# A transformer block with dilated local attention on one Trainium2 core: q and k columns in steps of four, V from a doubled scratch, halved reductions for late tiles, and a new order

## The chip, the cores and the metric

The kernel runs on one core of a Trainium2 chip. Its engines work on their own lists of instructions and meet at semaphores: TensorE (PE; its weight loads are listed apart as PEld), VectorE (DVE), ScalarE (ACT), GpSimd (POOL) and SyncE (SP), which here issues nearly all DMAs. The metric is device time of one execution in microseconds (us). Three runs of the kernel before gave 239.56, 240.42 and 240.76; their median, 240.42 us, is the time before.

## What is computed

One adaLN-conditioned block over S = 2048 tokens of D = 512: layer norm and modulation, attention with 32 heads of 16 dims in which each token sees itself and seven earlier tokens two apart, a gated residual, a second layer norm and modulation, a SwiGLU FFN of width 1792, a second gated residual.

```python
qkv = (h @ wqkv) ...                 # (B, H, S, 16) each
idx = pos[:, None] - arange(8) * 2   # window 8, dilation 2
logits = einsum('bhsd,bhswd->bhsw', q, kg) * scale   # masked where idx < 0
o = einsum('bhsw,bhswd->bhsd', softmax(logits), vg)
x = x + ga * (o @ wo)
h = layernorm(x) * (1 + cb) + sb
x = x + gb * ((silu(h @ w1) * (h @ w3)) @ w2)
```

All data is bf16; sums on TensorE are in float32.

## The kernel before

**How the work is staged.** The tokens are 16 tiles T of 128. A layer norm on DVE (statistics, L579) and ACT or DVE (normalization) is followed by a transpose and the modulation (`ln_T`; on PE for early groups, by DMA transpose and L648 on ACT for late ones). The normalized tokens lie as h with features on partitions. `proj_qk` computes q and k of up to four tiles as four chunks `ft` of 128 features on partitions by tokens (L722), with wqkv as the stationary operand; ACT copies them to the q buffer (L730) and to `kT` (L733, L734). `proj_v` computes V with tokens on partitions (L749), ACT copies it with dims ahead of heads (L759), and a DMA stores it in DRAM, in `v_scratch_dram`, one row of 512 per token.

**Attention of a tile** runs on DVE and PE:
- `logits`: one product of q with eight shifted views of kT (L780, 128x4096, the op called pq). PE sums the 16 features of a head with 0/1 matrices `E_sb[:, ft, :]`, one for each chunk, since chunk ft holds heads 8 ft to 8 ft + 7: four chunks by four column tiles of the array, 16 matmuls of 256 columns (L791, the op lg), out on partitions as (token block, head).
- `shift`, `exps`, `softmax`, for two tiles at a time: maximum (L803) and subtraction (L808) on DVE, exponential on ACT (L821), sum (L833), reciprocal (L835), normalization (L836) and a 32x32 block transpose (L840) on DVE, which puts (token, offset) on partitions.
- `values`: four DMAs of 256 KB per tile fetch V again, as 16 token pairs by 8 offsets on the partitions and two tokens in a row (128 packets of 2 KB each). DVE multiplies it by the weights in place (L862, 128x4096, the op av). PE sums the eight offsets with the 0/1 matrices `ind[:, r]` (8 matmuls of 512 columns in four column tiles, L871, the op ac), ACT copies (L877), a DMA transposes, PE applies wo (L895, the op wo), and DVE adds to x (L899, the op rs).

**The rest.** The second layer norm (`ln_sums`: L610, L614 and L625 on ACT, L620 and L621 on POOL, L622), then the FFN in groups of tiles [0, 1], [2, 3], [4..7], [8..11], [12..15]: `ffn_unit` is four matmuls for the gate and four for the up part (L911), silu on ACT (L917), the product on DVE (L922 or, in the last group, L925); `ffn_w2` the second matmul (L953, and L941 for the last two tiles), then L969 adds x and a DMA stores the result. DVE also scales wo and w2 by the gates (L987, L996). The gates come from two small matmul groups and a cast on DVE (`gate`, L555, L561).

**What sets the order.** `_build` makes 1151 operations, each with an engine, a planner's cost in ns (C_PQ, C_RED, `c_mm` and so on), what it reads and writes, and a key. `ORDER` (L1018) is a written-out permutation of them; each engine works its operations in that order, SP its DMAs too. `SLOTS` (L1064) says which buffer each value takes: the products and the fetched V share four buffers and two places in memory that is free by then (their names in the profile, sb_pq, sb_vsh, sb_vshq, sb_vshx, tell the buffer and not the use). `synchronize` puts in the waits that follow from both. Both lists were searched on the planner's costs outside the kernel. So an operation is found in the trace by its line and by its place in its engine's list.

Of the kernel before, what the change touches and what calls it, by code (L numbers as in the profile page):

```python
# [10 lines left out]
P = 128  # L11
# [10 lines left out]
PAD = 16  # L22
# [52 lines left out]
class Program:  # L75
# [41 lines left out]
    def dma(self, out, in_, key, packets, r=(), w=(), part=(), after=(), eng="sp", cost=450, group=None, transpose=False,  # L117
            store=False, again=False, pre=()):
        nc = self.nc

        def fn(e):
            a = out() if callable(out) else out
            b = in_() if callable(in_) else in_
            with nc.allow_non_contiguous_dma(reason="layout"):
                for pa, pb in pre:
                    e.dma_start(pa, pb).then_inc(o.inc[0], 16)
                return e.dma_start(a, b, transpose=True) if transpose else e.dma_start(a, b)
# [3 lines left out]
        ns = 600 if transpose else each * ((PACKET if pre == () and not SHIFTED else 84) if again else packet_ns(size)) + 170 * len(pre)  # L131
        o = self.op(eng, fn, cost, key, r=r, w=w, part=part, after=after, dma=(each, ns, *((900, 200) if store else (1300, 600))))
        o.count = 1 + len(pre)
# [119 lines left out]
C_PQ, C_RED, C_ACC, C_TINY = 2203, 440, 864, 90  # L253
# [18 lines left out]
SHIFTED = False  # L272
NWARM = 15
DMA_T = (4, 2)
AVCOL = frozenset(range(16))
# [5 lines left out]
def _build(p, A_x, A_wqkv, A_wo, B_w1, B_w3, B_w2, c, w_mod, out):  # L281
# [15 lines left out]
    kT = sb([P, KT, PAD + S], bf, "kT")  # L297
# [16 lines left out]
    E_sb = sb([P, KT, H], bf, "E")  # L314
    ones = sb([P, 512], bf, "ones")
    ind = sb([P, 2, 16, 2], bf, "ind")
# [27 lines left out]
    zrow = at([PAD, D], bf, "zrow", 25600)  # L344
# [7 lines left out]
    v_dram = nc.dram_tensor("v_scratch_dram", (PAD + S, D), bf)  # L352
    skew = nc.dram_tensor("skew_dram", (NT, 16, 4160), bf) if SHIFTED else None
# [20 lines left out]
    def held(pool, items):  # L374

        vals = []
        for i, item in enumerate(items):
# [9 lines left out]
    vc, vident, vcst, vE, vind, vbefore = (Val(n) for n in ("const", "ident", "cst", "E", "ind", "before"))  # L387
# [11 lines left out]
    p.op("pool", lambda e: e.memset(E_sb[:], 1.0), 150, k, w=[vE])  # L399
    p.op("pool", lambda e: e.affine_select(out=E_sb[:], in_=E_sb[:], compare_op=ALU.is_ge, fill=0.0, base=0,  # L400
                                           pattern=[[128, KT], [-16, H]], channel_multiplier=1), 320, k, w=[vE])
    p.op("pool", lambda e: e.affine_select(out=E_sb[:], in_=E_sb[:], compare_op=ALU.is_ge, fill=0.0, base=15,
                                           pattern=[[-128, KT], [16, H]], channel_multiplier=-1), 320, k, w=[vE])
    p.op("pool", lambda e: e.memset(ind[:], 0.0), 100, k, w=[vind])
    for r in range(2):
        p.op("pool", lambda e, r=r: e.memset(ind[:, r, :, r], 1.0), 100, k, w=[vind])
    for edge, mult in ((0, 1), (W - 1, -1)):
        p.op("pool", lambda e, edge=edge, mult=mult: e.affine_select(
            out=ind[:], in_=ind[:], compare_op=ALU.is_ge, fill=0.0, base=edge, pattern=[[0, 2], [-W * mult, 16], [0, 2]],
            channel_multiplier=mult), 250, k, w=[vind])  # L410
# [6 lines left out]
    p.op("dve", lambda e: e.memset(kT[:, :, 0:PAD], 0.0), 120, k, w=[vkpad])  # L417
# [35 lines left out]
    p.dma(v_dram[0:PAD, :], zrow[:], ("load", 11), (16, 1024), r=[vzrow] + wm_hold, w=[vvpad], store=True)  # L453
# [52 lines left out]
    def first_modulation(part):  # L506
# [16 lines left out]
        if not part:  # L523
# [3 lines left out]
            def kbias(e):  # L527
                for ft in range(KT):
                    for t in range(KT):
                        ins = e.matmul(bank(vb)[:, ft:ft + 1], wqkv[:, t, D + ft * P:D + (ft + 1) * P], sab[:, t:t + 1],  # L530
                                       start=(t == 0), stop=(t == KT - 1))
# [176 lines left out]
    def proj_qk(gi, Ts, kind, vh):  # L708
# [7 lines left out]
        for ft in range(KT):  # L716
# [3 lines left out]
            def mm(e, ts, ft=ft, vp=vp):  # L720
                for t in ts:
                    ins = e.matmul(bank(vp)[:, 0:n], wqkv[:, t, kind * D + ft * P:kind * D + (ft + 1) * P], vh.at[:, t, 0:n],  # L722
# [5 lines left out]
            def ev(e, ft=ft, vp=vp):  # L728
                if kind == 0:
                    return e.activation(dstv.at[:, ft, at0:at0 + n], bank(vp)[:, 0:n], ACT.Copy, scale=SCALE)  # L730
                to = kT[:, ft, PAD + 512 * cch + at0:PAD + 512 * cch + at0 + n]
# [11 lines left out]
    def proj_v(T, tt, vh):  # L743
# [19 lines left out]
        p.dma(v_dram[PAD + T * P:PAD + (T + 1) * P, :], lambda: vt.at[:], k, (128, 1024), r=[vt], w=[vd], cost=400, store=True)  # L763
# [5 lines left out]
    def logits(Ts):  # L769

        vl = Val("ps_l", psum)
        for i, T in enumerate(Ts):
# [4 lines left out]
            def prod(e, T=T, cch=cch, tt=tt, vp=vp):  # L777
                in0 = bass.AP(vq[cch].at, tt * P, [[KT * 512, P], [0, W], [512, KT], [1, P]])
                in1 = bass.AP(kT, PAD + T * P, [[KT * (PAD + S), P], [-DIL, W], [PAD + S, KT], [1, P]])
                return e.tensor_tensor(bass.AP(vp.at, 0, [[8 * D, P], [KT * P, W], [P, KT], [1, P]]), in0, in1, ALU.mult)  # L780

            prods[T] = p.op("dve", prod, C_PQ, ("pq", T), r=[vq[cch]] + ks + (q_hold if cch < 2 else []), w=[vp], lock=True)
            def red(e, i=i, T=T, vp=vp):
                c0 = vl.at * 512 + i * W * 32
                if T == 0:
# [3 lines left out]
                for ft in range(KT):  # L789
                    for q in range(4):  # L790
                        ins = e.matmul(PALL[32 * q:32 * q + 32, c0:c0 + W * 32], E_sb[:, ft, :], bass.AP(vp.at, ft * P + 8 * q, [[W * KT * P, P], [KT * P, W], [32, 4], [1, 8]]),  # L791
                                       start=(ft == 0 and (T > 0 or q > 1)), stop=(ft == KT - 1), tile_position=(0, 32 * q))
                return ins

            p.op("pe", red, C_RED + (110 if T == 0 else 0), ("lg", T), r=[vp, vE] + ([vbefore, vc] if T == 0 else []), part=[vl], tiled=True)
# [32 lines left out]
    def softmax(Ts, vl, ve, vx_):  # L828
# [7 lines left out]
        p.op("dve", lambda e: e.tensor_tensor(ve.at[0][:, 0:n], bass.AP(PALL, bank(vl).offset, [[8 * 512, P], [W * 32, n], [1, 32], [32, W]]),  # L836
                                              bass.AP(ve.at[2], 0, [[64, P], [32, n], [1, 32], [0, W]]), ALU.mult),
# [272 lines left out]
```

## Time and profile before

| | |
|---|---|
| runs | 239.56, 240.42, 240.76 us |
| median | 240.42 us |
| span of the profiled execution | 237.7 us (237.65 by its windows) |
| around the span, against the median | 2.77 us |
| matmuls (PE records) | 1665, busy 229.9 us |
| DVE | 284 instructions, busy 169.8 us |
| ACT | 311 instructions, busy 156.4 us |
| DMA | 38.31 MB, mean 161 GB/s |

The execution's own time is not listed apart from its span; what lies around the span is put at the difference to the median. The profile is one execution; a group of it lists line, engine, operation, output<-input, count, then busy us and mean ns of one, then the engine's idle time just before and what ended it. "Busy" of PE is modelled: a 512-column matmul is drawn 379 ns long although the next one starts some 216 ns later. In the windows view each engine has its busy time in that stretch. In the chain of waits each piece is what the next one waited for.

### The profile page before, as it was taken

What the parts mean: (1) busy time and instruction counts of PE and PEld (TensorE: products, weight loads), DVE (VectorE), ACT (ScalarE), POOL (GpSimd) and SP (SyncE); (2) the same over time, 40 slices, a digit from 0 to 9 for tenths busy, and PEclk for the clock granted to TensorE, in tenths of its full rate; (3) what the DMA queues carried; (4) which work ended last, traced back from release to release, by engine and by line L of the source; (5) the groups of instructions that cost most, each with busy time, mean ns of one, the idle gap of its engine ahead of it and who ended that gap; (6) DMA issues with size and microseconds to landing.
All of it is one profiled execution on the core that took longest, in us unless ns stands there. A gap on an engine that the chain in (4) does not pass through costs nothing.

```text
span 237.7 us, 4314 instructions
## 1 busy us (share of the span) xinstructions
PE 229.9 (97%) x1665; PEld 120.7 (51%) x1689; DVE 169.8 (71%) x284; ACT 156.4 (66%) x311; POOL 23.1 (10%) x55
## 2 busy tenths in 40 slices
PE   7899998999999999999999999999999999999996
PEld 2667543544568855754434444444344444444454
DVE  4789998999999999999999847379134424042722
ACT  2289798899989987683689799444757926133100
POOL 8323050001001000030000021000001100000000
PEclk9999999999999999999999999999999999999999
DMA  6999999989999977693897484330032142000002
GB/s 185 341 352 351 238 274 179 188 221 297 327 261 273 285 181 223 139 261 69 205 330 116 124 229 105 103 117 0 3 90 88 44 77 80 0 0 0 3 0 88
DMA packets 44731, 38.31 MB, mean 161 GB/s; under 512 B 19736, under 2 KB 36008, under 8 KB 44712
## 3 DMA queue, kind: packets, MB, share of 16 engines
q1 hardware_dynamic: 44656, 38.04, 63.3%
q8 instruction: 13, 0.21, 0.4%
q14 instruction: 6, 0.05, 0.1%
q10 hardware_dynamic: 56, 0.01, 0.0%
HBM read 29.63 MB, written 4.21 MB: 142 GB/s over the span
## 4 chain that ended last, share of the span: by engine, by line
PE 68%; DVE 12%; DMA 7%; ACT 7%; issue 3%; POOL 1%; SPq 1%; DVEq 0%
PE pall L911 38%; PE pall L953 13%; PE pall L722 5%; DMA sb_wo<-in_A_wo_dram 5%; PE pall L895 4%; DVE sb_vsh L862 3%; PE pall L941 3%; DMA sb_wm_s<-in_w_mod_dram 2%; PE pall L871 2%; PE pall L749 2%; ACT sb_h L648 1%; ACT sb_xn L614 1%; PE pall L791 1%; DVE sb_pq L780 1%; DVE sb_pq L862 1%
## 5 line engine op out<-in xcount | busy, mean ns | idle before, releaser
L911 PE MATMUL pall<-sb_h,sb_w 128*128 128x512 bf16 (+1 forms) x554 | 99.6, 336 | 0.5 <-issue 0.2
L911 PEld LDWEIGHTS pall<-sb_h,sb_w 128*128 128x128 bf16 x560 | 52.2, 98 | 47.1 <-ACT sb_sg L917 5.2
L917 ACT ACTIVATE sb_sg<-pall 128x512 bf16<-128x512 f32 (+1 forms) x70 | 33.9, 516 | 29.6 <-PE pall L911 28.6
L953 PE MATMUL pall<-sb_w,sb_hh 128*128 128x512 bf16 x190 | 43.4, 379 | 0.3
L722 PE MATMUL pall<-sb_h,sb_wqkv 128*128 128x512 bf16 (+1 forms) x157 | 30.4, 336 | 1.3 <-ACT sb_v L759 0.8
L953 PEld LDWEIGHTS pall<-sb_w,sb_hh 128*128 128x128 bf16 x196 | 18.9, 98 | 22.7 <-issue 0.4
L921 ACT ACTIVATE sb_hh<-pall 128x256 bf16<-128x256 f32 (+1 forms) x56 | 26.8, 497 | 3.4 <-PE pall L911 3.0
L922 DVE TENSOR_TENSOR sb_hh<-sb_sg,sb_hh 128x256 bf16<-128x256 bf16 (+1 forms) x56 | 17.7, 351 | 12.8 <-ACT sb_hh L921 12.8
L969 DVE TENSOR_TENSOR sb_o<-pall,sb_x 128x512 bf16<-128x512 f32 (+3 forms) x18 | 10.9, 627 | 18.5 <-PE pall L953 13.7
L722 PEld LDWEIGHTS pall<-sb_h,sb_wqkv 128*128 128x128 bf16 x160 | 14.6, 98 | 14.0 <-ACT sb_v L759 1.3
L925 DVE TENSOR_TENSOR sb_hh<-sb_sg,pall 128x512 bf16<-128x512 bf16 x14 | 9.1, 684 | 16.0 <-PE pall L911 15.9
L648 ACT ACTIVATE sb_h<-sb_h,sb_modc 128x512 bf16<-128x512 bf16 x16 | 11.7, 806 | 11.2 <-DMA sb_h<-sb_xn 11.2
L620 POOL TENSOR_SCALAR sb_rs<-sb_var 128x2 f32<-128x2 f32 x8 | 3.4, 427 | 144.4 <-ACT sb_xn L614 144.4
L862 DVE TENSOR_TENSOR sb_pq<-sb_pq,sb_al 128x4096 bf16<-128x4096 bf16 x7 | 15.8, 2285 | 1.0 <-DMA sb_pq<-v_scratch_dram 1.0
L862 DVE TENSOR_TENSOR sb_vsh<-sb_vsh,sb_al 128x4096 bf16<-128x4096 bf16 x7 | 15.9, 2281 | 0.0
L749 PE MATMUL pall<-sb_wqkv,sb_h 128*128 128x512 bf16 x59 | 15.2, 379 | 0.3 <-issue 0.2
L895 PE MATMUL pall<-sb_wo,sb_ot 128*128 128x512 bf16 x60 | 14.9, 379 | 0.6 <-issue 0.5
L673 ACT ACTIVATE sb_h<-pall,sb_modc 128x256 bf16<-128x256 bf16 (+1 forms) x20 | 12.2, 659 | 2.7 <-DVE sb_modc L522 1.8
L780 DVE TENSOR_TENSOR sb_vsh<-sb_q,sb_kT 128x4096 bf16<-128x4096 bf16 x6 | 13.6, 2286 | 0.4 <-ACT sb_q L730 0.4
L625 ACT ACTIVATE sb_xn<-sb_x,sb_nb,sb_rs 128x512 bf16<-128x512 bf16 x16 | 12.4, 818 | 1.9 <-DVE sb_nb L622 1.7
L614 ACT ACTIVATE sb_xn<-sb_x,sb_nm 128x512 bf16<-128x512 bf16 x16 | 11.4, 716 | 2.7 <-DVE sb_nm L610 2.7
L899 DVE SCALAR_TENSOR_TENSOR sb_x<-pall,sb_x 128x512 bf16<-128x512 f32 x16 | 10.7, 678 | 2.9 <-PE pall L895 2.7
(111 smaller groups left out, 254.5 us busy)
## 6 DMA issues: line engine op xcount, KB each, us to landing
sb_pq<-v_scratch_dram SPq DMA_DIRECT2D x28, 256.0 KB, 6.8
sb_vsh<-v_scratch_dram SPq DMA_DIRECT2D x28, 256.0 KB, 5.0
sb_w<-in_B_w_dram SPq DMA_DIRECT2D x6, 512.0 KB, 6.9
sb_w<-in_B_w_dram SPq DMA_DIRECT2D x6, 384.0 KB, 5.9
v_scratch_dram<-sb_v SPq DMA_DIRECT2D x16, 128.0 KB, 5.8
out_dram<-sb_o SPq DMA_DIRECT2D x14, 128.0 KB, 1.8
sb_wqkv<-in_A_wqkv_dram SPq DMA_DIRECT2D x6, 256.0 KB, 6.2
sb_x<-in_A_x_dram SPq DMA_DIRECT2D x3, 512.0 KB, 7.7
```

The costliest lines, as they stand in the source:

```text
L614: p.op("act", lambda e, vn=vn, T=T: e.activation(vn.at[:], x_sb[:, T, :], ACT.Square, bias=nm[:, T, :], scale=D ** -0.5, accum_out=var[:, ...
L648: return e.activation(vh.at[:, ft, 0:n * P], vh.at[:, ft, 0:n * P], ACT.Identity, bias=modc[:, 8 * which + ft:8 * which + ft + 1], scale=m ...
L722: ins = e.matmul(bank(vp)[:, 0:n], wqkv[:, t, kind * D + ft * P:kind * D + (ft + 1) * P], vh.at[:, t, 0:n], start=(t == ORDER[0]), stop=(t ...
L749: ins = e.matmul(bank(vp), vh.at[:, t, tt * P:(tt + 1) * P], wqkv[:, t, 2 * D:3 * D], start=(t == ORDER[0]), stop=(t == ORDER[-1]))
L780: return e.tensor_tensor(bass.AP(vp.at, 0, [[8 * D, P], [KT * P, W], [P, KT], [1, P]]), in0, in1, ALU.mult)
L862: return e.tensor_tensor(v_w, v_w, a_w, ALU.mult)
L895: ins = e.matmul(bank(vy), vt.at[:, ft, :], wo[:, ft, :], start=(ft == 0), stop=(ft == KT - 1))
L911: ins = e.matmul(bank(vp)[:, 0:n], wt[:, t, fi * P:(fi + 1) * P], vh.at[:, t, 0:n], start=(t == 0), stop=(t == KT - 1))
L917: p.op("act", lambda e: e.activation(vt.at[:, 0:n], bank(vgp)[:, 0:n], ACT.Silu), c_act(n), k, r=[vgp], w=[vt], table="silu")
L921: p.op("act", lambda e: e.activation(vh_.at[:, 0:n], bank(vup)[:, 0:n], ACT.Copy), c_act(n), k, r=[vup], w=[vh_])
L922: p.op("dve", lambda e: e.tensor_tensor(vh_.at[:, 0:n], vt.at[:, 0:n], vh_.at[:, 0:n], ALU.mult), 60 + n * 69 // 128, k, r=[vt], w=[vh_], ...
L953: ins = e.matmul(bank(vz), vhh[fi].at[:, tt * P:(tt + 1) * P], w2[:, fi, :], start=(fi == 0), stop=(fi == NF - 1))
```

## The change

1. **q and k columns in steps of four.** The stationary operand of chunk ft is now columns ft, ft + 4, ft + 8 and so on of wqkv in place of 128 neighbouring ones; the bias matmuls of the first group likewise (L530). Partition p of each chunk then holds head p // 4. One 128x32 matrix `ind` (1 where p // 4 is the head) takes the place of the four in `E_sb` and of the two in `ind[:, r]`; five of eight building operations on POOL go.
2. **V as 32 tokens by 4 offsets.** The scratch has two columns of 512 per row: row r holds V of token r and of token r + 32, so each store writes every row twice (256 packets of 1 KB in place of 128). Each of the four loads per tile is 32 tokens by 4 offsets on partitions with two token blocks in a row, still 128 packets of 2 KB. Slots 0 to 3 of the fetched V are offsets 0 to 3, slots 4 to 7 offsets 4 to 7.
3. **The normalization** (L836) is done per tile, two instructions of 256 elements a partition in place of one of 512, writing in the order that the transpose needs; the block transpose then reads and writes contiguous rows.
4. **Halves added on VectorE.** For tiles 12 to 15 (`PREL`) a DVE add folds chunks 2 and 3 of the products onto 0 and 1, and the reduction has 8 matmuls in place of 16. For tiles 10 to 15 (`PREA`) a DVE add folds offsets 4 to 7 of the weighted V onto 0 to 3, and the reduction has 4 matmuls in place of 8.
5. **A new searched order** and new buffer slots for the now 1164 operations. Read as lists: PE starts with 14 warm-up matmuls in a row, does all q and k of tiles 0 to 3 ahead of most of V; SP fetches the second gate's weights early; DVE has both gate casts ahead of the first product; the logits of tiles 14 and 15 come after the value reduction of tile 11, the folded products of tiles 13 to 15 ahead of it.

Branches that were never taken (`SHIFTED`, tiles outside `AVCOL`) are removed with it.

```diff
-                    ins = e.matmul(bank(vp)[:, 0:n], wqkv[:, t, kind * D + ft * P:kind * D + (ft + 1) * P], vh.at[:, t, 0:n],
+                    ins = e.matmul(bank(vp)[:, 0:n], wqkv[:, t, kind * D + ft:(kind + 1) * D:KT], vh.at[:, t, 0:n],
...
-        p.dma(v_dram[PAD + T * P:PAD + (T + 1) * P, :], lambda: vt.at[:], k, (128, 1024), r=[vt], w=[vd], cost=400, store=True)
+        p.dma(bass.AP(v_dram, (PAD + T * P) * 2 * D, [[2 * D, P], [D - 64 * D, 2], [1, D]]),
+              lambda: bass.AP(vt.at, 0, [[D, P], [0, 2], [1, D]]), k, (256, 1024), r=[vt], w=[vd], cost=400, store=True)
...
+            if T in PREL:
+                def fold(e, vp=vp):
+                    lo, hi = (bass.AP(vp.at, j * 2 * P, [[8 * D, P], [KT * P, W], [1, 2 * P]]) for j in range(2))
+                    return e.tensor_tensor(lo, lo, hi, ALU.add)
+
+                p.op("dve", fold, C_ADD, ("pq", T), w=[vp], lock=True)
...
+                last = (2 if T in PREL else KT) - 1
-                for ft in range(KT):
+                for ft in range(last + 1):
                     for q in range(4):
-                        ins = e.matmul(PALL[32 * q:32 * q + 32, c0:c0 + W * 32], E_sb[:, ft, :], bass.AP(vp.at, ft * P + 8 * q, [[W * KT * P, P], [KT * P, W], [32, 4], [1, 8]]),
+                        ins = e.matmul(PALL[32 * q:32 * q + 32, c0:c0 + W * 32], ind[:],
+                                       bass.AP(vp.at, ft * P + 8 * q, [[W * KT * P, P], [KT * P, W], [32, 4], [1, 8]]),
...
-        p.op("dve", lambda e: e.tensor_tensor(ve.at[0][:, 0:n], bass.AP(PALL, bank(vl).offset, [[8 * 512, P], [W * 32, n], [1, 32], [32, W]]),
-                                              bass.AP(ve.at[2], 0, [[64, P], [32, n], [1, 32], [0, W]]), ALU.mult),
+        for i in range(n):
+            def norm(e, i=i):
+                src = bass.AP(PALL, bank(vl).offset + i * W * 32, [[8 * 512, P], [128, 2], [1, 32], [32, 4]])
+                rec = bass.AP(ve.at[2], i * 32, [[64, P], [0, 2], [1, 32], [0, 4]])
+                dst = bass.AP(ve.at[0], i * W * 32, [[2 * W * 32, P], [128, 2], [4, 32], [1, 4]])
+                return e.tensor_tensor(dst, src, rec, ALU.mult)
...
-        for q in range(4):
-            p.dma(lambda q=q: vv.at[:, 2 * q:2 * q + 2, :],
-                  bass.AP(v_dram, (PAD + T * P + 32 * q) * D, [[2 * D, 16], [-DIL * D, W], [1, 2 * D]]), ("vl", T), (128, 2048),
+        for wh in range(2):
+            for c in range(2):
+                p.dma(lambda s=4 * wh + 2 * c: vv.at[:, s:s + 2, :],
+                      bass.AP(v_dram, (PAD + T * P + 64 * c - 4 * DIL * wh) * 2 * D, [[2 * D, 32], [-DIL * 2 * D, 4], [1, 2 * D]]),
...
+        if T in PREA:
+            p.op("dve", lambda e: e.tensor_tensor(vv.at[:, 0:4, :], vv.at[:, 0:4, :], vv.at[:, 4:8, :], ALU.add), C_ADD, ("av", T),
+                 w=[vv], lock=True)
...
+            parts = 1 if T in PREA else 2
+            for wh in range(parts):
+                for q in range(4):
+                    ins = e.matmul(b[32 * q:32 * q + 32, :], ind[:], vv.at[:, 4 * wh + q, :], start=(wh == 0), stop=(wh == parts - 1),
+                                   tile_position=(0, 32 * q))
```

More of the change, by code (lines that the diff above doesn't have):

```diff
@@ L21 @@
 NF = F // P
-PAD = 16
+PAD = 32
+KPAD = 16
 EPS = 1e-5
@@ L891, in values @@
+        p.op("act", lambda e: e.activation(va.at[:], bank(vo), ACT.Copy), c_act(512), ("ac", T), r=[vo], w=[va])
+        p.dma(lambda: vt.at[:], lambda: va.at[:], ("ac", T), (128, 1024), r=[va], w=[vt], cost=1250, transpose=True)
         vy = Val("ps_y", psum)
```

101 lines of the change are left out of this document (35 added, 66 removed), and 120 rows, old and new, of tables (ORDER, SLOTS).

## The prediction, made before the result

> **What bounds the kernel now.** I read the page first: its busy shares and the strip of 40 slices (5.94 us each).
>
> ```profile
> span 237.7 us, 4314 instructions
> ...
> PE 229.9 (97%) x1665; PEld 120.7 (51%) x1689; DVE 169.8 (71%) x284; ACT 156.4 (66%) x311; POOL 23.1 (10%) x55
> ```
> ```profile
> PE   7899998999999999999999999999999999999996
> ...
> DVE  4789998999999999999999847379134424042722
> ```
>
> TensorE (PE) is busy from end to end, so less matmul work can pay. But VectorE (DVE) stands at 8 or 9 from slice 2 to slice 22 (to 137 us) and only then falls off. Its 71% is a mean over a full half and an idle one. So I cut the span with the windows view: at the first q·k product (23.60), at the value reduction of tile 11 (132.90), and at the start of the FFN of tiles 8 to 11 (157.01). Columns: length, then busy time of PE, PEld, DVE, ACT, POOL.
>
> ```profile
> 0.00:23.60 23.60, 21.11 (x198) 13.14 (x201) 16.92 (x58) 13.67 (x32) 10.55 (x35) 1.00 0.96 308
> 23.60:132.90 109.30, 107.02 (x951) 61.30 (x961) 106.43 (x139) 89.99 (x185) 8.51 (x12) 1.00 0.94 223
> 132.90:157.01 24.11, 23.84 (x121) 10.38 (x117) 13.53 (x34) 19.28 (x34) 2.15 (x4) 1.00 0.59 157
> ```
>
> In the middle stretch PE is idle 2.28 us of 109.30 and DVE 2.87 us: two engines are full side by side. Behind it PE is full and DVE half idle. The clock is 1.00 throughout. The cut at 132.90 is where they meet, as the timeline shows:
>
> ```profile
> 130.56 2.29 DVE L862 TENSOR_TENSOR sb_pq<-sb_pq,sb_al 128x4096 bf16<-128x4096 bf16 x1
> ```
> ```profile
> 132.90 0.61 PE L871 MATMUL pall<-sb_pq,sb_ind 128*32 128x512 bf16 x8
> ```
>
> DVE ends tile 11's weighting at 132.85; PE starts on it at 132.90. There is no slack there. The chain of waits says the same 18 us earlier (start, length, what):
>
> ```profile
> 112.24 2.21 DVE sb_vshx L780
> ...
> 114.50 0.62 PE pall L791 x16
> ...
> 132.19 0.87 PE pall L791 x32
> 133.06 0.46 PE pall L871 x8
> ...
> 134.49 5.18 PE pall L911 x24
> ...
> 170.13 1.84 PE pall L871 x32
> ```
>
> Up to here the chain is on DVE, from here nearly all on PE. So a change that takes work from PE and gives it to DVE has to be booked on both sides of 132.9.
>
> **The change, part by part.**
>
> *Halved reductions (PE).* Tiles 12 to 15 get 8 in place of 16 matmuls for the logits, tiles 10 to 15 get 4 in place of 8 for the values. In the chain 32 logit matmuls (two tiles) take 0.87, so 0.435 a tile; 32 value matmuls (four tiles) take 1.84, so 0.46 a tile. Saved: 4 x 0.22 + 6 x 0.23 = 2.26 us.
>
> *Folds and split (DVE).* Ten adds of 128 x 2048 bf16 are new, and each of the eight normalizations becomes two of 256 elements. Rows of the groups:
>
> ```profile
> L996 DVE TENSOR_TENSOR sb_w<-sb_w,sb_gb_bc 128x2048 bf16<-128x2048 bf16 x2 | 2.4, 1191 | 0.0
> L836 DVE TENSOR_TENSOR sb_attn<-pall,sb_ssum 128x512 bf16<-128x512 f32 x8 | 5.5, 687 | 0.1
> L969 DVE TENSOR_TENSOR sb_o<-pall,sb_x 128x256 bf16<-128x256 f32 x2 | 0.8, 420 | 1.1 <-PE pall L941 1.1
> L922 DVE TENSOR_TENSOR sb_hh<-sb_sg,sb_hh 128x512 bf16<-128x512 bf16 x28 | 10.6, 419 | 12.8 <-ACT sb_hh L921 12.8
> L803 DVE TENSOR_REDUCE sb_mx<-pall 128x64 f32<-128x512 f32 x8 | 5.4, 680 | 0.0
> L808 DVE TENSOR_TENSOR pall<-pall,sb_mx 128x512 f32<-128x512 f32 x8 | 5.6, 697 | 0.1
> L899 DVE SCALAR_TENSOR_TENSOR sb_x<-pall,sb_x 128x512 bf16<-128x512 f32 x16 | 10.7, 678 | 2.9 <-PE pall L895 2.7
> ```
>
> One operation overlaps the next by about 0.08 (a product lasts 2.29 but takes 2.21 in the chain), so a fold costs 1.19 - 0.08 = 1.11 and a split 2 x 0.34 - 0.61 = 0.07. In all DVE gains 10 x 1.11 + 8 x 0.07 = 11.7 us. A fold could take between half a product (1.10) and the two-tensor row (1.19); I take 1.11.
>
> *The new order*, read as two lists. I counted which operations stand on each side of tile 11's value reduction.
> DVE, from the first product to tile 11's weighting and its fold: six of the ten folds (6.7), six splits (0.4), two more FFN products (0.7), but one pair of maximum and subtraction fewer (1.2), one residual add fewer (0.6) and some tiny ones (0.2): 5.8 us more.
> PE, from that reduction to the end: 24 FFN matmuls fewer (5.18 by the chain's row for 24), five halved value reductions (5 x 0.23), but the halved logits of tiles 14 and 15 now follow it (0.43): 5.9 us less. Ahead of it PE has 5.9 - 2.26 = 3.6 us more.
> So by PE alone the reduction starts at 132.9 + 3.6 = 136.5; by DVE alone, from the same first product and with the same idle time, at 132.85 + 5.8 = 138.65. What follows takes 237.65 - 132.90 - 5.9 = 98.85. **If PE sets the pace, the end is at 235.35 (2.3 less); if DVE does, at 237.5 (0.15 less).** The gain is what DVE can start earlier.
>
> *The early part.* The first product waited for the last q:
>
> ```profile
> 23.60 2.29 DVE L780 TENSOR_TENSOR sb_vsh<-sb_q,sb_kT 128x4096 bf16<-128x4096 bf16 x1 [0.45 <-ACT sb_q L730]
> ```
>
> The new PE list does q and k of tiles 0 to 3 before nearly all of v, so this wait goes. Late next on DVE are the two gate casts now queued ahead of the first product. All of DVE's list stands behind them. They need both gate loads, which end the 5.6 MB at the head of SP's list; the window to 23.60 moves 308 GB/s, so 18.2 us and the first transfers' 2 us, then the gates on PE. I put the first product at 22.6, 1.0 earlier (between none and 2.0), hence the reduction at 137.65.
>
> *Column order of q and k.* The weights of these matmuls are read four elements apart, which no row shows. The nearest rows:
>
> ```profile
> 11.66 0.56 PEld L530 LDWEIGHTS pall<-sb_sab,sb_wqkv 128*128 128x128 bf16 x16
> ```
> ```profile
> 14.16 1.92 PE L722 MATMUL pall<-sb_h,sb_wqkv 128*128 128x256 bf16 x16
> ```
>
> Packed loads with almost no matmul behind them take 35 ns each; a 256-column matmul takes 120. Spread loads cost nothing as long as they stay under that cover: I take 0. If each took four times as long (140), the 64 matmuls of tiles 0 to 3 lose 0.02 each and the 16 bare bias loads 0.105 each: 3.0 us, all ahead of the first product. The 512-column ones (0.216) stay covered. A gain is excluded: a load under cover has nothing to give.
> [...]
>
> *V twice.* Each of the 16 stores writes 256 KB in place of 128; the four loads per tile keep their 128 packets of 2 KB.
>
> ```profile
> v_scratch_dram<-sb_v SPq DMA_DIRECT2D x16, 128.0 KB, 5.8
> ```
> ```profile
> DVE sb_pq L862 <- DMA sb_pq<-v_scratch_dram: 1.0, 1, 1.0
> ```
>
> At 223 GB/s 128 KB more are 0.6 us of queue time a store. Three stand before the first weighting's loads (1.8), against a first weighting now wanted earlier; the wait that was 1.0 I leave at 1.0, since SP issues two other loads fewer in between. SP works its list in order, so weights and transposes wait behind a load that waits for a store. Bounds of DVE's wait: 0 and 2.8, so -1.0 to +1.8.
>
> *Second layer norm.* Between the last output projection of a group and its FFN, PE now has 64 matmuls, 13.8 us, for tiles 8 to 11 and for 12 to 15. Before:
>
> ```profile
> 139.67 1.85 PE pall L895 x8
> ```
> ```profile
> 182.92 1.24 PE pall L895 x5
> ```
> ```profile
> 152.98 2.93 ACT L648 ACTIVATE sb_h<-sb_h,sb_modc 128x512 bf16<-128x512 bf16 x4 [3.01 <-DMA sb_h<-sb_xn]
> ```
> ```profile
> 195.82 2.93 ACT L648 ACTIVATE sb_h<-sb_h,sb_modc 128x512 bf16<-128x512 bf16 x4 [4.71 <-DMA sb_h<-sb_xn]
> ```
> ```profile
> 191.18 0.58 SPq L127 DMA_DIRECT2D out_dram<-sb_o  x1
> ```
> ```profile
> 198.80 1.41 PEld L911 LDWEIGHTS pall<-sb_h,sb_w 128*128 128x128 bf16 x8 [0.46 <-ACT sb_h L648]
> ```
>
> The chain through statistics, transposes and modulation took 155.91 - 141.52 = 14.4 and 198.75 - 184.16 = 14.6. Unchanged it would be 0.6 + 0.8 = 1.4 late. But the store that split the last four transposes (0.58) is out of their way and ScalarE's list is denser there; I take 0.3 (bounds 0 and 1.4).
>
> Free: fewer constants (POOL busy 10%), one table for the reductions in place of four (loads of the same 128x32 form), the contiguous transpose, SP's list (166 issues both times).
>
> *Sum*, on the profiled execution: 137.65 + 98.85 + 0.3 = 236.8, that is 0.85 under its 237.65. The runs' median of 240.42 lies 2.77 above this span (the execution's own time is not given apart from it): **239.6 us.**
>
> **Rivals.**
> 1. *DVE keeps up*: first product 2 us earlier or 2 us of its 2.87 idle gone, no late norm; then PE sets the pace: 136.5 + 98.85 + 2.77 = 238.1. For it: DVE's idle time in the middle is mostly single waits, like the 1.0 above. Against: two engines at 97% seldom both lose their gaps.
> 2. *The doubled stores make DVE wait* (slower): place, the first weightings, around 35 us, where the loads queue behind three doubled stores on SP. Their landing then sets DVE's pace, so an earlier first product brings nothing (1.0 lost), and the wait grows by 1.8: both go one for one down the DVE path to tile 11, 239.6 + 2.8 = 242.4. Slower than before from 0.85 on. For it: DMA share 0.94 to 132.9. Against: by 30 us the queue has had time to drain.
> 3. *Spread weights break the cover* (slower): 3.0 on PE ahead of the first product: 242.6. It begins at about 120 ns a load and outweighs the gain at 0.85 in all.
> 4. *The halving doesn't halve*: a lone group of 8 costs as much as of 16. Then 2.26 comes back, of it 0.7 on the side where DVE leads anyway: 239.6 + 1.6 = 241.2. Against it: 0.435 is four rounds of 256 columns with nothing over.
>
> **How the numbers follow.** My sum, 238.6 to 240.6: 0.50. Rival 1, 0.22; rival 2, 0.14; rival 3, 0.09; rival 4, 0.05. A measurement of this kernel can tell about 0.5% (1.2 us) from no change. Faster by more (under 239.2) is rival 1 and three tenths of my sum: 0.37. Within: the rest of my sum and the rest of rival 4: 0.38. Slower (over 241.6): rivals 2 and 3 and two fifths of 4: 0.25. Range: 237.6 to 242.6; outside lie a gain beyond PE's 2.3 and two of the slow cases together.
>
> **What would show it.** Right: PE busy about 2 us less; DVE about 12 more, most after 133 in the strip; logit groups of 8 matmuls in 0.22 steps; the value reduction of tile 11 between 136.5 and 139 just behind a DVE fold; the first product before 23. Wrong: q and k matmuls of 256 columns further apart than 0.12; DVE waiting over 2 us for v_scratch_dram; PE idle before the last two FFN groups by over 1 us.

## The result, and the profile after

| | before | after |
|---|---|---|
| median (lowest to highest) | 239.99 us (239.48 to 240.76), 4 runs | 243.69 us (242.62 to 244.28), 4 runs |
| ratio, 95% interval | | 1.014 (1.0101 to 1.0179) |
| span of the profiled execution | 237.65 us | 242.4 us |
| time of that execution | not listed | 244.28 us |
| time of an execution beyond its span, all runs listed | 2.2 to 2.3 us | 1.8 to 1.9 us |

The changed kernel is slower by 1.4%. The forecast was 239.6, with a range to 242.6. The profiled execution is the longest of the four (their spans are 240.7 to 242.4). The page of the changed kernel, with the strips of PE and DVE:

```profile
span 242.4 us, 4229 instructions
...
PE 228.7 (94%) x1610; PEld 123.4 (51%) x1633; DVE 182.9 (75%) x302; ACT 156.6 (65%) x311; POOL 21.6 (9%) x50
...
PE   7899799999799999989998999989999999999995
...
DVE  6599699998899999988999987979925412315613
```

PE has less to do than before (229.9), DVE 13.1 us more (about 12 was forecast). But PE's strip, which before had nines from slice 7 on up to the last, now has sevens and eights in slices 4, 10, 17, 21 and 26 (6.06 us each, counted from 0). The windows view, cut as in the forecast: at the first product, at tile 11's value reduction, at the FFN of tiles 8 to 11 (length, then busy time of PE, PEld, DVE, ACT, POOL). The last line ends at tile 11's fold in place of its reduction:

```profile
0.00:22.16 22.16, 19.56 (x206) 14.16 (x209) 17.15 (x59) 12.22 (x29) 8.92 (x30) 1.00 0.88 277
22.16:142.41 120.25, 113.16 (x917) 64.25 (x927) 113.96 (x150) 94.98 (x194) 9.00 (x13) 1.00 0.84 231
142.41:162.67 20.26, 19.10 (x103) 8.42 (x105) 16.85 (x38) 15.83 (x27) 1.85 (x4) 1.00 0.62 166
...
22.16:141.41 119.25, 112.16 (x911) 63.95 (x922) 113.00 (x149) 94.35 (x193) 9.00 (x13) 1.00 0.85 232
```

The middle stretch is 120.25 long, where the forecast had 137.65 - 22.6 = 115.05 and before had 109.30. PE is idle 7.09 us of it (2.28 before), DVE 6.29 (2.87): **two engines that were full side by side now both have gaps.** PE's waits, summed by what ended them (total, times, longest), of the changed kernel and then of the kernel before, whose list is nearly empty behind the start:

```profile
PE pall L533 <- DVE sb_ones L387: 1.5, 1, 1.5
PE pall L879 <- DVE sb_pq L866: 1.5, 1, 1.5
PE pall L654 <- ACT sb_xn L587: 1.4, 1, 1.4
PE pall L891 <- DMA sb_ot<-sb_oa: 1.2, 1, 1.2
PE pall L907 <- ACT sb_sg L913: 1.1, 2, 0.8
PE pall L505 <- DMA sb_wm_s<-in_w_mod_dram: 1.0, 2, 0.7
PE pall L907 <- ACT sb_h L639: 0.7, 1, 0.7
PE pall L879 <- ACT sb_oa L885: 0.6, 1, 0.6
```
```profile
PE pall L542 <- DVE sb_ones L389: 1.5, 1, 1.5
PE pall L722 <- ACT sb_v L759: 0.8, 1, 0.8
PE pall L663 <- DVE sb_xn L600: 0.6, 1, 0.6
```

No single wait explains 3.7 us: these are many waits of at most 1.5 us, for VectorE, ScalarE and DMAs. What the change does to the folds and the halved groups is as forecast, as the timelines at tile 11 show (DVE, then PE):

```profile
137.65 2.29 DVE L866 TENSOR_TENSOR sb_pq<-sb_pq,sb_al 128x4096 bf16<-128x4096 bf16 x1
...
140.19 1.22 DVE L870 TENSOR_TENSOR sb_pq<-sb_pq 128x2048 bf16<-128x2048 bf16 x1
```
```profile
138.85 3.63 PE L907 MATMUL pall<-sb_h,sb_w 128*128 128x512 bf16 x16
142.41 0.40 PE L879 MATMUL pall<-sb_pq,sb_ind 128*32 128x512 bf16 x4
142.63 0.39 PE L791 MATMUL pall<-sb_vsh,sb_ind 128*32 128x256 bf16 x8
142.85 0.39 PE L791 MATMUL pall<-sb_pq,sb_ind 128*32 128x256 bf16 x8
```

A halved group takes 0.22 and a fold lasts 1.22. But the reduction starts at 142.41, not 137.65, and 1.0 after its fold: PE was still at 16 FFN matmuls, so here PE came last and not DVE.

### The profile page after: what moved, and what is told of

Same layout as the page of the kernel before. It is cut to its first block, busy times and chain, and to the rows that moved or that the text cites. A ratio compares the mean times of both kernels' runs of the same rounds, so it can differ in the third digit from the quotient of the medians.

```text
span 242.4 us, 4229 instructions
## 1 busy us (share of the span) xinstructions
PE 228.7 (94%) x1610; PEld 123.4 (51%) x1633; DVE 182.9 (75%) x302; ACT 156.6 (65%) x311; POOL 21.6 (9%) x50
## 4 chain that ended last, share of the span: by engine, by line
PE 49%; DVE 19%; DMA 12%; ACT 10%; SPq 5%; POOL 3%; issue 1%; ACTq 0%
PE pall L907 33%; PE pall L949 9%; SPq L126 5%; DMA v_scratch_dram<-sb_v 5%; DVE sb_pq L772 4%; DMA sb_h<-sb_xn 3%; DMA sb_x<-in_A_x_dram 3%; PE pall L937 3%; DVE sb_st L570 2%; DVE sb_vsh L772 2%; ACT sb_xn L605 2%; PE pall L891 2%; DMA sb_ot<-sb_oa 2%; POOL sb_rs L577 2%; ACT sb_xn L616 2%
## 5 line engine op out<-in xcount | busy, mean ns | idle before, releaser
L907 PEld LDWEIGHTS pall<-sb_h,sb_w 128*128 128x128 bf16 x560 | 53.5, 98 | 47.7 <-ACT sb_sg L913 4.0
L713 PE MATMUL pall<-sb_h,sb_wqkv 128*128 128x512 bf16 (+1 forms) x154 | 29.7, 335 | 0.6 <-DMA sb_w<-in_B_w_dram 0.2
L917 ACT ACTIVATE sb_hh<-pall 128x256 bf16<-128x256 f32 (+1 forms) x56 | 26.2, 498 | 6.2 <-PE pall L907 6.2
L918 DVE TENSOR_TENSOR sb_hh<-sb_sg,sb_hh 128x256 bf16<-128x256 bf16 (+1 forms) x56 | 18.3, 348 | 8.9 <-ACT sb_hh L917 8.0
L713 PEld LDWEIGHTS pall<-sb_h,sb_wqkv 128*128 128x128 bf16 x160 | 17.1, 114 | 9.2 <-ACT sb_kT L725 0.4
L772 DVE TENSOR_TENSOR sb_pq<-sb_q,sb_kT 128x4096 bf16<-128x4096 bf16 x9 | 20.5, 2282 | 0.0
L866 DVE TENSOR_TENSOR sb_pq<-sb_pq,sb_al 128x4096 bf16<-128x4096 bf16 x5 | 11.4, 2287 | 1.4 <-DMA sb_pq<-v_scratch_dram 1.2
L866 DVE TENSOR_TENSOR sb_vsh<-sb_vsh,sb_al 128x4096 bf16<-128x4096 bf16 x5 | 11.4, 2284 | 0.0
L772 DVE TENSOR_TENSOR sb_vsh<-sb_q,sb_kT 128x4096 bf16<-128x4096 bf16 x5 | 11.4, 2282 | 0.0
```

The source lines that it names most:

```text
L713: ins = e.matmul(bank(vp)[:, 0:n], wqkv[:, t, kind * D + ft:(kind + 1) * D:KT], vh.at[:, t, 0:n], start=(t == ORDER[0]), stop=(t == ORDER[ ...
L866: return e.tensor_tensor(v_w, v_w, a_w, ALU.mult)
L907: ins = e.matmul(bank(vp)[:, 0:n], wt[:, t, fi * P:(fi + 1) * P], vh.at[:, t, 0:n], start=(t == 0), stop=(t == KT - 1))
L917: p.op("act", lambda e: e.activation(vh_.at[:, 0:n], bank(vup)[:, 0:n], ACT.Copy), c_act(n), k, r=[vup], w=[vh_])
L918: p.op("dve", lambda e: e.tensor_tensor(vh_.at[:, 0:n], vt.at[:, 0:n], vh_.at[:, 0:n], ALU.mult), 60 + n * 69 // 128, k, r=[vt], w=[vh_], ...
```

## The experiments

Three theories. **D**: the folds and the split normalizations of the softmax (the expectations call them split or second layer norms) on VectorE set the pace. **V**: the doubled store does, by its landing and by holding SP's list. **O**: the new list itself, which lets engines wait for each other, whatever is in it. "List" is `ORDER` and `SLOTS` together; a kernel with the old list has the old buffer slots too. Every kernel was timed against the kernel before on the same chip; ratios are to it. "No folds" means that each fold is a memset of one column and each reduction is full.

### The list and the folds apart

**e1_old_order.** `ORDER` and `SLOTS` of the kernel before, each fold and each second half of a normalization right behind the step that it belongs to:

```diff
 ORDER = [
-    0, 68, 70, 69, 71, 62, 67, 66, 7, 8, 1, 2, 10, 4, 5, 3, 9, 61, 16, 65, 58, 60, 72, 64, 13, 6, 53, 54, 18, 17, 87, 82, 23, 20, 19, 22,
+    10, 15, 1, 5, 7, 8, 11, 6, 12, 4, 2, 16, 53, 3, 17, 18, 23, 19, 20, 26, 27, 0, 58, 59, 60, 61, 62, 82, 83, 84, 54, 55, 85, 63, 64, 65, 66,
...
```

> Everything of the change except its order: the list and the buffer slots of the kernel before, with each added fold and each second layer norm put right behind the step that it belongs to. Theory D (VectorE's 11.7 us of folds and split layer norms set the pace wherever they stand): about as slow as the changed kernel, 243 to 246, since the old list leaves no room for them. Theory V (the doubled store of V, by its landing and by holding SP's queue): 243 to 244, as the store is in it. Theory O (the new list, which lets engines wait for each other between the first product and tile 11's value reduction): 238 to 240.5.

Measured: 253.98 us, ratio 1.0634 (1.0555 to 1.0712). Slower than any theory said.

**e2_old_order_no_folds** and **e3_new_order_no_folds.** The first as e1, the second with the new list; both with these lines and the like for the folds of the weighted V (not shown):

```diff
+FOLDL = frozenset([])
+FOLDA = frozenset([])
...
-                def fold(e, vp=vp):
+                def fold(e, T=T, vp=vp):
+                    if T not in FOLDL:
+                        return e.memset(idle[:, T:T + 1], 0.0)
...
-                last = (2 if T in PREL else KT) - 1
+                last = (2 if T in FOLDL else KT) - 1
...
-            parts = 1 if T in PREA else 2
+            parts = 1 if T in FOLDA else 2
```

> As e1_old_order, but the folds are left out: each becomes a memset of one column on VectorE, and every tile's products are reduced in full on TensorE. What is left of the change is the layout of q, k and V, the doubled store and the split layer norm. Theory D: 239.5 to 240.5, as before. Theory V: 243 to 244. Theory O: 239.5 to 240.5. If both D and O hold in part, it stands below e1_old_order by what the folds cost in the old list.

> The changed kernel with its own list, but the folds left out as in e2_old_order_no_folds (a memset of one column, full reductions: TensorE has 2.3 us more to do, VectorE 11.1 us less). Theory D: 239 to 241. Theory V: 243 to 246. Theory O: 243 to 246, since the list stays.

Measured: e2 241.1 us, ratio 1.0047 (1.0014 to 1.0081); e3 246.28 us, ratio 1.0272 (1.0202 to 1.0341). e2 lies 0.6 above the 239.5 to 240.5 of D and O, well under V's 243; e3 lies 0.3 above the 243 to 246 of V and O, far from D's 239 to 241.

The four corners of list and folds (the changed kernel at the lower right was timed apart from the other three):

| | no folds | folds |
|---|---|---|
| old list | 241.1 | 253.98 |
| new list | 246.28 | 243.69 |

**The new list alone, order and buffer slots together, costs 5.2 us** (e3 against e2; about 3.5 to 7.2 by their intervals). No run here pairs the order of one list with the slots of the other, so the two are not told apart. In the new list the folds win 2.6 us (3.2 by the ratios, 1.3 to 5.1 by their intervals), about what they save on PE; in the old list they cost 12.9. Theory D falls: e3 has 11 us less on DVE than the changed kernel and is slower. The windows of e2, then of e3, show the same operations with other gaps:

```profile
0.00:22.00 22.00, 19.92 (x188) 13.12 (x191) 15.98 (x54) 12.21 (x27) 8.46 (x29) 1.00 0.93 297
22.00:50.00 28.00, 27.68 (x281) 15.81 (x287) 27.21 (x34) 25.51 (x47) 4.13 (x6) 1.00 0.85 262
50.00:105.00 55.00, 53.44 (x462) 35.16 (x460) 53.53 (x89) 46.89 (x112) 3.48 (x6) 1.00 0.86 268
105.00:150.00 45.00, 43.96 (x308) 19.71 (x311) 38.72 (x67) 34.94 (x62) 3.69 (x6) 1.00 0.69 170
```
```profile
0.00:22.00 22.00, 19.14 (x190) 13.35 (x192) 16.69 (x53) 11.65 (x28) 8.65 (x29) 1.00 0.88 278
22.00:50.00 28.00, 26.19 (x245) 14.29 (x250) 25.69 (x33) 23.99 (x43) 4.52 (x6) 1.00 0.80 225
50.00:105.00 55.00, 52.06 (x482) 34.45 (x483) 52.16 (x79) 45.20 (x106) 2.26 (x4) 1.00 0.86 254
105.00:150.00 45.00, 42.94 (x288) 19.72 (x295) 34.97 (x56) 31.85 (x57) 2.79 (x4) 1.00 0.74 187
```

To 150 us PE idles 5.0 us in e2 (2.08 + 0.32 + 1.56 + 1.04) and 9.7 in e3 (2.86 + 1.81 + 2.94 + 2.06), although e3's DVE is freer in three of the four stretches. Most of the changed kernel's longer waits stand in e3 too: 1.43 at 27.86 us (1.37 at 27.39 with folds), 1.08 at 105.69 (1.18 at 104.96), 0.66 at 132.75 (0.80 at 132.15). These come with the list and not with the folds. The one of 1.50 at 63.54 does not: there e3 has 0.18.

Why folds hurt the old list: there PE's reduction follows right behind DVE's product, and it now waits for the fold between them. Two lines of e1's PE, and its windows:

```profile
141.26 0.40 PE L879 MATMUL pall<-sb_pq,sb_ind 128*32 128x512 bf16 x4 [2.53 <-DVE sb_pq L870]
...
178.97 6.18 PE L907 MATMUL pall<-sb_h,sb_w 128*128 128x512 bf16 x19 [3.39 <-ACT sb_sg L913]
```
```profile
175.00:180.00 5.00, 1.56 (x7) 0.59 (x7) 4.96 (x5) 1.57 (x3) 0.00 (x0) 0.99 0.00 0
180.00:185.00 5.00, 5.00 (x17) 1.72 (x14) 1.65 (x2) 2.77 (x5) 0.00 (x0) 0.67 0.00 0
```

Behind the second wait the granted clock falls to 0.67 (mean of 180 to 185 us) and 19 matmuls take 6.18, 0.33 each in place of 0.22. So e1 pays twice, by waiting and by the clock; its PE is busy 232.8 us against 228.7 in the changed kernel with the same matmuls.

### V's store, the weights' columns, GpSimd, SP's list

**e4_v_stored_once.**

```diff
-        p.dma(bass.AP(v_dram, (PAD + T * P) * 2 * D, [[2 * D, P], [D - 64 * D, 2], [1, D]]),
-              lambda: bass.AP(vt.at, 0, [[D, P], [0, 2], [1, D]]), k, (256, 1024), r=[vt], w=[vd], cost=400, store=True)
+        p.dma(v_dram[PAD + T * P:PAD + (T + 1) * P, :], lambda: vt.at[:], k, (128, 1024), r=[vt], w=[vd], cost=400, store=True)
```

> The changed kernel, its list and its folds, with V stored once (128 KB a tile) and read with the loads of the kernel before, so that V's rows do not stand beside the weights that they are multiplied by: it computes other values, and only its time is read. Theory D: 243 to 244. Theory V: 239.5 to 241, and VectorE's waits for V's scratch at 60 us and ScalarE's at 58 to 66 us are gone. Theory O: 242.5 to 244.

Measured: 244.16 us, ratio 1.0216 (1.0144 to 1.0288). Theory V falls: with half the bytes the time stays, and e2, which stores V twice, was at 241.1.

**g4_before_store_twice** and **g3_before_spread_weights**, one part each in the kernel before:

```diff
-        p.dma(v_dram[PAD + T * P:PAD + (T + 1) * P, :], lambda: vt.at[:], k, (128, 1024),
+        p.dma(bass.AP(v_dram, (PAD + T * P) * D, [[D, P], [(PAD + S) * D, 2], [1, D]]),
+              lambda: bass.AP(vt.at, 0, [[D, P], [0, 2], [1, D]]), k, (256, 1024),
```
```diff
-                    ins = e.matmul(bank(vp)[:, 0:n], wqkv[:, t, kind * D + ft * P:kind * D + (ft + 1) * P], vh.at[:, t, 0:n],
+                    ins = e.matmul(bank(vp)[:, 0:n], wqkv[:, t, kind * D + ft:(kind + 1) * D:KT], vh.at[:, t, 0:n],
```

> The kernel before with one part alone: each tile of V is stored twice (256 KB, the second copy into a region that nothing reads). The forecast's term is 0: 239.6 to 240.4. Its second rival, by which the longer stores make VectorE wait at the first weightings: 241.5 to 242.5, with VectorE idle over 1.5 us for V's scratch between 30 and 60 us.

> The kernel before with one part of the change alone: the columns of the q and k weights are read in steps of four (so q and k hold other columns, the same ones, in each tile; the first reduction then sums other products, and only the time is read). The forecast's term is 0: 239.6 to 240.4. Its third rival, by which the spread loads break the cover of the matmuls: 241.2 to 243. A load of 43 in place of 35 ns in the bias group, seen in the changed kernel, would give 0.2 us at most.

Measured: g4 241.01 us, ratio 1.0041 (1.0008 to 1.0075); g3 240.72 us, ratio 1.0032 (0.9996 to 1.0068). Both lie a little above the forecast's 0 (g3's interval includes it) and under its rivals. **c0_old_list_layout_only** has all three layout parts (and no folds, no memsets) in the old list:

```diff
-PREL = frozenset(range(12,16))
-PREA = frozenset(range(10,16))
+PREL = frozenset()
+PREA = frozenset()
```

> The change without its folds and without its order: layout of q, k and V, the doubled store and the split layer norms in the list of the kernel before, with no memsets in place of the folds (e2_old_order_no_folds had ten, and 1.2 us more on VectorE). The terms e, f and g of the forecast: +0.3, 239.7 to 240.6. If g3_before_spread_weights and g4_before_store_twice add up: 241 to 241.8.

Measured: 240.63 us, ratio 1.0027 (0.9996 to 1.0059): 0.6 us, not told from 0. The sum of g3 and g4 would be 1.8; with intervals this wide, it is not shown whether the two add up. In g3 the 16 bias matmuls with spread weights took

```profile
13.09 0.67 PE L530 MATMUL pall<-sb_sab,sb_wqkv 128*128 128x1 bf16 x16
```

0.67, where packed ones took 0.54: 0.1 us.

**f3_nb_before_product.** In the changed kernel GpSimd's step at 22.59 lasts 1.92, and DVE and PE wait for it (GpSimd, DVE, PE):

```profile
22.59 1.92 POOL L575 TENSOR_SCALAR sb_rs<-sb_mv 128x2 f32<-128x2 f32 x1
```
```profile
22.16 2.28 DVE L772 TENSOR_TENSOR sb_pq<-sb_q,sb_kT 128x4096 bf16<-128x4096 bf16 x1
26.32 0.30 DVE L582 SCALAR_TENSOR_TENSOR sb_nb<-sb_mv,sb_rs 128x2 f32<-128x2 f32 x3 [1.88 <-POOL sb_rs L577]
```
```profile
27.39 0.29 PE L654 MATMUL pall<-sb_ident,sb_xn 128*128 128x128 bf16 x2 [1.37 <-ACT sb_xn L587]
```

The edit moves the product (entry 387) behind those small DVE steps in `ORDER`:

```diff
-387, 266, 268, 267, 324, 275,
+266, 268, 267, 324, 275, 387,
```

> The changed kernel with the first product moved behind the three small VectorE steps that wait for GpSimd (it would start at about 24.7 us in place of 22.16), so that GpSimd is not slowed beside it. If TensorE's wait of 1.37 us at 27.4 us is a price of the list that is paid to the end: 242.2 to 243.2. If VectorE's late start counts (its second product then ends at about 29.3 us, 0.5 later): 244 to 245.5.

Measured: 244.05 us, ratio 1.0169 (1.0104 to 1.0235), as before the edit. GpSimd's four such steps now take 0.22 each and PE's 1.37 is gone, but PE waits at the next meeting point. PE of f3, then two of its DVE lines, and the eighth product in the changed kernel:

```profile
29.25 0.62 PE L791 MATMUL pall<-sb_pq,sb_ind 128*32 128x256 bf16 x16 [1.48 <-DVE sb_pq L772]
```
```profile
24.71 4.49 DVE L772 TENSOR_TENSOR sb_pq<-sb_q,sb_kT 128x4096 bf16<-128x4096 bf16 x2
...
55.62 2.28 DVE L772 TENSOR_TENSOR sb_pq<-sb_q,sb_kT 128x4096 bf16<-128x4096 bf16 x1
```
```profile
55.50 2.28 DVE L772 TENSOR_TENSOR sb_pq<-sb_q,sb_kT 128x4096 bf16<-128x4096 bf16 x1
```

The first product starts 2.55 us later (24.71 for 22.16) and the eighth 0.12 later: **a late first product is caught up within eight products.** The time alone would also fit the low end of the second range, 244 to 245.5, where the late start counts; the trace speaks against that. The forecast's "the gain is what DVE can start earlier" has no price that shows here.

**f2_weights_before_wait.** SP's loads 41, 47 and 48 move up in `ORDER`, around 53 us:

```diff
-203, 434, 433, 442, 444, 441, 443, 407, 417, 41, 47, 48, 259, 42,
+203, 41, 47, 48, 434, 433, 442, 444, 441, 443, 407, 417, 259, 42,
```

> The changed kernel with three entries of SP's list moved up: the loads of the FFN's weights that stood behind tile 3's loads of V (issued at 56.5 us) go out ahead of SP's wait for tile 3's stored V (51.3 to 53.5 us). Theory O, by which the new list's waits cost what each of them shows: VectorE's wait for V at 60 us (1.21 us), TensorE's at 63.5 us (1.50) and ScalarE's for the store at 65.9 us (1.11) shrink, 242.2 to 243.2. If VectorE's load sets the pace instead, the 1.2 us of its wait are what is won: 242.4 to 243. If a stall that goes in this list only lets the next one grow: 243.4 to 244.

Measured: 246.37 us, ratio 1.0261 (1.0155 to 1.0367): slower, which no theory had. Two of its four executions took 244.6 us with the mean granted clock at 1.000, just above the last range of 243.4 to 244; the other two took 248.1 and 248.2 at 0.986. The profile is of one of these. DVE waits longer for V, PE behind it, and the clock falls (DVE, PE, windows of f2):

```profile
60.74 2.29 DVE L866 TENSOR_TENSOR sb_vsh<-sb_vsh,sb_al 128x4096 bf16<-128x4096 bf16 x1 [2.95 <-DMA sb_vsh<-v_scratch_dram]
```
```profile
63.09 0.61 PE L879 MATMUL pall<-sb_vsh,sb_ind 128*32 128x512 bf16 x8 [1.46 <-DVE sb_vsh L866]
65.56 1.05 PE L879 MATMUL pall<-sb_pq,sb_ind 128*32 128x512 bf16 x8 [1.85 <-DVE sb_pq L866]
```
```profile
60.00:65.00 5.00, 2.25 (x46) 1.19 (x44) 4.08 (x2) 3.06 (x7) 0.00 (x0) 0.91 0.62 223
65.00:70.00 5.00, 4.10 (x20) 1.97 (x22) 4.93 (x6) 3.11 (x6) 0.00 (x0) 0.50 0.31 79
...
64.00:65.00 1.00, 0.00 (x0) 0.00 (x0) 1.00 (x1) 0.35 (x1) 0.00 (x0) 0.56 0.09 32
```

With three loads of weights ahead of it the second pair of V's loads into `sb_vsh` goes out at 52.18 us in place of 50.17: a place in SP's list is paid by another.

### Which stretch of the new list loses the time

Lists were mixed. **h0_new_list_other_buffers** is the control for buffers; **h1** and **h2** take the old list first. The kernels have the lists written out; the rule, with NEW and OLD for the two lists, is

```python
ORDER = OLD[:n] + [i for i in NEW if i not in OLD[:n]]
```

with n = 0 (h0), 415 (h1), 612 (h2) and each value in the free buffer that was left longest ago.

> A control for the two that follow: the changed kernel, its list and its folds, with the buffers given out anew along the list (each value takes the free buffer that was left longest ago) in place of the searched buffer numbers. If the buffer numbers matter little: 243 to 245, with TensorE's idle time in the same places as in the changed kernel. If they are part of what the search found: 246 or more.

> The changed kernel with the list of the kernel before up to the product of tile 7 (64.55 us in e2_old_order_no_folds; no fold stands in it) and the new list for the rest; buffers as in h0_new_list_other_buffers. Theory O, each stretch of the new list keeps what it loses: TensorE's idle time of the first 60 us is 2 us less, so 241 to 242.5. A rival, by which the early waits cost nothing because the start of the late products is set by something else: 243.5 to 245.

> As h1_old_list_to_pq7, with the old list up to the product of tile 12, the first that is folded (99 us in e2_old_order_no_folds). Theory O: another 1.5 us less, 239.5 to 241.5; what is left above 238 is what the new list loses after 100 us. The rival: 243.5 to 245.

Measured: h0 253.37 us, ratio 1.0549 (1.0456 to 1.0641); h1 255.27, 1.0621 (1.0532 to 1.0709); h2 253.62, 1.0534 (1.0449 to 1.062). The buffer numbers alone are worth 10 us (h0 against the changed kernel): in h0 PE waits 3.4 us for a bank that DVE has not read yet,

```profile
PE pall L907 <- DVE sb_o L965: 3.4, 1, 3.4
```

so h1 and h2 say nothing on the lists. **h4** (n = 446) and **h5** (n = 743, no folds ahead of the seam) keep the searched buffers but for six values; **h6, h7, h8** put the new list first (n = 359, 713, 908; OLD and NEW exchanged), no folds, a few values moved.

> The changed kernel, folds and all, with the list and the buffers of the kernel before for its first 446 entries (some 66 us), and the new list with its own buffers behind; six values had to take another buffer. Theory O, each stretch of the new list loses time for good: TensorE's idle time of the first 70 us is 2 to 3.4 us less, 240 to 241.8. A rival, by which the early waits cost nothing and the loss is all behind: 243 to 244.5.

> As h4_old_list_first_66us, but with the old list and buffers for 743 entries (some 112 us), and with folds only where they stand behind that (products of tiles 14 and 15, weighted values of tiles 10 to 15; the folds of tiles 12 and 13 become a memset of one column and their reductions are full). Theory O: the new list's idle time before 112 us goes, eight of ten halved reductions stay: 239.5 to 241. If the loss is that VectorE has no room for the folds behind 112 us: 243 or more.

> e2_old_order_no_folds with the new list and its buffers for the first 359 entries (some 50 us), the old list behind; no folds. Theory O, what TensorE idles in a stretch is lost for good: TensorE idles 2.3 us more before 50 us in e3_new_order_no_folds than in e2_old_order_no_folds, so 243 to 244. The rival, by which an early wait is made up for at the next place where the engines meet: 240.5 to 242.

> The same with 713 entries (some 105 us). Theory O: 3.7 us of idle time more, 244 to 245.5. The rival with the loss behind 105 us: 240.5 to 242.

> The same with 908 entries (some 150 us). Theory O: 4.7 us more, 245 to 246.5, about the whole loss. The rival with the loss in the last stretch: 241 to 243; with the loss between 105 and 150 us: 244.5 to 246.5, and then h7_new_list_first_105us at 240.5 to 242.

Measured: h4 244.71 us, ratio 1.0175 (1.0115 to 1.0236); h5 248.66, 1.0357 (1.0301 to 1.0414); h6 255.03, 1.0627 (1.0552 to 1.0703); h7 248.77, 1.0374 (1.0291 to 1.0458); h8 252.15, 1.0502 (1.0446 to 1.0559). h4 is the clean one and a miss for theory O in its simple form: PE idles 1.5 us less than in the changed kernel up to 50 us, yet the ninth product starts at 65.96 us for 66.06 and nothing is won at the end, as in f3. h6, h7 and h8 miss every range given, and h5 is in its "243 or more". The medians of these four are above both lists whole (the intervals of h5 and h7 overlap e3's), and new waits stand in them. The longest of h5 and of h6, 8 us behind their seams:

```profile
PE pall L897 <- DVE sb_o L971: 4.9, 1, 4.9
```
```profile
PE pall L897 <- ACT sb_kT L728: 6.4, 1, 6.4
```

So the stretch stays open, and with it which of the list's waits make up the 5.2 us. What is shown is that these lists and their buffers could not be cut at any of the places tried without a loss, and that a wait ahead of 60 us is not simply added to the end.

### Folds where VectorE stands idle

**c1_old_list_late_folds.** In e2, DVE idles 5.1 us behind the last weighting. Only the values of tiles 12 to 15 are folded, there; two reductions go back by two FFN groups:

```diff
-PREL = frozenset(range(12,16))
-PREA = frozenset(range(10,16))
+PREL = frozenset()
+PREA = frozenset(range(12,16))
...
```

> As c0_old_list_layout_only, with the folds of the weighted values of tiles 12 to 15 alone, put into the 5.1 us in which VectorE stands idle behind the last weighting (168.1 to 173.3 us in e2_old_order_no_folds), two reductions moved back by two FFN groups. If a fold that lies in idle time of VectorE pays what the halved reduction saves on TensorE (4 times 0.43 us): 1.7 us under c0. If it delays what stands behind it: the same as c0, or slower.

Measured: 239.8 us, ratio 0.9995 (0.9963 to 1.0028), 0.8 us under c0 (0.0 to 1.5 by the spread of 12 runs each). The expected 1.7 was mis-sized when it was written: 0.43 is the whole group of 8, so four halvings save about 4 x 0.22 = 0.88, and what came agrees. The DVE list shows the folds in the gap (an FFN product follows 0.52 after them):

```profile
164.49 2.28 DVE L866 TENSOR_TENSOR sb_vsh<-sb_vsh,sb_al 128x4096 bf16<-128x4096 bf16 x1
166.69 1.21 DVE L870 TENSOR_TENSOR sb_pq<-sb_pq 128x2048 bf16<-128x2048 bf16 x1
167.82 2.35 DVE L870 TENSOR_TENSOR sb_vsh<-sb_vsh 128x2048 bf16<-128x2048 bf16 x2
170.09 1.21 DVE L870 TENSOR_TENSOR sb_pq<-sb_pq 128x2048 bf16<-128x2048 bf16 x1
```

It pays about what the layout costs and no more: equal to the kernel before. No kernel here beats that one.

## Why the prediction was wrong, by its steps

- **The step that failed** is in the new order: "by DVE alone, from the same first product and with the same idle time, at 132.85 + 5.8 = 138.65". The idle time did not stay. From the first product to the end of tile 11's fold (141.41) DVE idled 6.25 us against 2.87 before: 3.4 more, where the forecast had 0. It worked 113.00 against 106.43: 6.6 more, for the 5.8 counted. With the first product 0.4 earlier than forecast, that makes the fold 3.8 late. Then DVE was not the last at this point: the reduction waited another 1.0 for PE. By PE's own account up to there it worked 132.72 us (19.56 + 113.16) against 128.13 before, 4.6 more (forecast 3.6), and idled 9.69 against 4.77, 4.9 more (forecast 0). So the reduction came 9.5 us later than before, of which the forecast had 4.75. e3 and e2 show that the list, with its slots, does this: 5.2 us with no fold in either. Counting what stands on each side of a point prices the work in a list, not its fit.
- **The early part** was right in size (first product at 22.16, forecast 22.6), but no gain at the end shows for it: f3, h4. The 2 us of the first transfers stand in the windows of the kernel before: its DMAs moved 0 GB/s from 0 to 1 us, 32 from 1 to 2 and 262 from 2 to 3.
- **VectorE's load** over the whole span grew by 13.1 us for the 11.7 counted. e3 shows that it did not set the pace.
- **Halved reductions** were right: 0.22 for the halved groups, 2.26 in all against 2.6 between e3 and the changed kernel. Rival 4 is out.
- **Column order**: q and k matmuls stayed 0.12 apart (16 in 1.91), the bare bias loads cost 0.1 more (16 loads took 0.69 in the changed kernel, 43 ns each, for 0.56 before); g3's 0.8 us is not told from 0. Rival 3 is out.
- **V twice**: 1.0 us alone (g4, 0.2 to 1.8), within its bounds, not the 0 taken. Rival 2 asked for 2.8 by a wait of DVE: that wait was 1.2, and e4 without the second copy is as slow.
- **Second layer norm**: PE waited 0.68 ahead of the FFN of tiles 8 to 11; what follows tile 11's reduction took 99.99, 0.84 above the forecast's 99.15.
- **The sum**: 236.8 of span against 242.4; 4.76 of the miss lie ahead of that reduction, 0.84 behind it. The term of 2.77 set the median of several runs against the span of one execution; beyond its own span the profiled execution of the changed kernel took 1.88 (244.28 - 242.4), so in time the miss is 4.7 for that execution and 4.1 for the median. A rival "the new list fits worse" was missing, and the range had no room for it.

## What to carry to other kernels

Where two engines are full side by side under a written-out order, a new order is a change of its own: before pricing what it carries, count the idle time that it can lose, here 5 us against 2.3 us of saved matmuls. What work moved to another engine is worth depends on where it stands: it paid in a hole of that engine's list (c1: 0.8 us) and in the list that was searched with it (2.6 us), and cost a multiple where it came between the other engine's steps (e1: 13 us). A wait seen early in a trace is not a loss at the end until an edit that removes it has moved the end.

## What the runs showed of the hardware

- **The granted clock fell around pauses of PE, to 0.50 in f2, but not in every execution.** In e1 its mean is 0.99 from 175 to 180 us, where PE waits 3.39, then 0.67 from 180 to 185 and 1.00 from 185 to 190. In f2 it falls inside the second of two waits (1.46 and 1.85 us with only 8 matmuls between; 0.56 from 64 to 65 us) and is 0.50 from 65 to 70 us. Two of f2's four executions have a mean clock of 1.000, so no such fall, and are 3.5 us shorter. In h7 five single waits of 1.4 to 1.7 us left the mean clock of the profiled execution at 1.000. The single waits of up to 1.5 us in the kernels before and after left it at 1.00. How long a pause it takes is not shown.
- **One GpSimd step took 1.92 us beside a VectorE product and 0.22 without.** In the changed kernel, the step that started 0.43 after the product lasted 1.92, to 24.51, just behind the product's end at 24.44; without the product beside it, in f3, it took 0.22. What holds it is not shown. No cost to the whole kernel shows: f3, without it, is no faster (244.05 us for 243.69).
